# Centring the rows as they leave PSUM, whole-height transposing products, other gate sums for three pairs, and a new order

## Chip, core and metric

The kernel runs on one core of a Trainium2 chip. The metric is the device time of one execution in microseconds. The kernel before took 188.77 us, the median of three runs (188.55 to 188.9). The engines named below are PE (TensorE: matrix products), DVE (VectorE), ACT (ScalarE), POOL (GpSimd) and SP, whose queue issues nearly all transfers.

## What is computed

Four batches of eight heads, each a complex gated linear recurrence over 768 tokens of width 48, followed by a layer norm and a two-layer network over the 384 joined columns:

```
mag = np.sqrt(a_re * a_re + a_im * a_im)
scale = np.minimum(mag, 0.999) / (mag + 1e-06)
...
for t in range(S):
    new_re = ar * S_re - ai * S_im
    new_im = ar * S_im + ai * S_re
    kv = np.einsum('bhd,bhe->bhde', k[:, :, t], v[:, :, t])
    S_re, S_im = (new_re + kv, new_im)
    y[:, :, t] = np.einsum('bhd,bhde->bhe', q[:, :, t], S_re)
...
mu = np.mean(x, axis=-1, keepdims=True)
var = np.mean((x - mu) ** 2, axis=-1, keepdims=True)
xn = (x - mu) / np.sqrt(var + 1e-06) * g_ln
ch = np.maximum(xn @ w_ch1, 0.0) @ w_ch2
return (x + ch).astype(np.float32)
```

## The kernel before

The tokens are cut into 24 chunks of 128 (index `n`), taken two at a time as 12 pairs (`P`), three pairs to a batch. For a pair the gates come first: `are` and `aim` are loaded, ACT takes a logarithm and a reciprocal (`ln`, `iv`), DVE or POOL form the ratio `r` and its square `r2`, and `u`, `l`, `lc` give the log of the decay, `th` the angle. PE sums both along the tokens with triangular matrices of ones, `dec` (L466) and `ph` (L481): a partition holds two neighbouring tokens (`j` 0 and 1), so each of the two chunks of a pair needs two products with `u_e` or `u_th`. `ph` starts with a product that brings in the carried angle. ACT turns the sums into `e`, `en`, `sin`, `cos`. Then `ke`, `qe`, `ks`, `qs` scale keys and queries; `kT` and `qT` (L581) are PE transposes of eight heads, copied out as `ksT`, `qsT`. Some chunks take a transposing DMA on SP instead. `am` (L604) makes the scores, DVE masks them (`atm`), `gm` and `G` carry the state, and `y` (L665) is the output of the recurrence. `dps` (L563) moves the last decay row into a column: eight products with one moving column, whose rows are partitions 96 to 127. `decc` copies it out.

For the network, `x` (L677) copies `y` out of PSUM as bf16 on ACT or DVE, `bn` (L680) takes mean and variance of `x` on DVE, and `xtr`, `xT` transpose it. The mean is taken out through the first weights: `wp` (L375) forms the column means of the scaled weights on PE, and `wc` (L381) scales `w1b` and subtracts them. That is done once. `mm1` (L718) multiplies, in six halves to a pair; `relu` leaves PSUM on ACT or DVE; `mm2` (L744) multiplies again, in three parts to a chunk. `ot` scales by `rstd` and adds `x`: in one DVE operation from PSUM (L761), or as `oa` on ACT (L751) followed by an addition on POOL (L759). `st` stores.

`warm` products at the start compute nothing that is used.

`PLAN` (L39) is a written-out list of all operations. An operation `name:E` goes to the queue of engine `E` in the order of the list, a digit after it names its PSUM bank, and `@other` makes it wait for `other`, so that POOL and DVE take turns. Each engine works through its own queue in order. `RINGS` says how many buffers a tile has.

Of the kernel before, what the change touches and what calls it, by code (L numbers as in the profile page):

```python
# [9 lines left out]
FP32 = mybir.dt.float32  # L10
# [24 lines left out]

ENGINES = {"P": "PE", "A": "ACT", "V": "DVE", "G": "POOL", "S": "SP"}
# [27 lines left out]
sin.3.0:A6 are.5.0:S mm1.0.1.1:P0 atm.3:V2 wl.1:G@mm1.0.1.0 v.1:A qt.3.0:P6 vf.2.0:S relu.0.1:A0 ke.2.0.0:G wc.2.2:V5
gm.2:P2 y.2:P3 G.2:V2 cos.3.0:A6 ke.2.0.1:G mm1.0.2.0:P0 wc.0.2:V4 x.2:A3 y.3:P5 qe.2.0.0:G wc.0.0:V4 gm.3:P2 x.3:A5
mm1.0.2.1:P0 wc.0.1:V4 ks.2.0.1:G xtr.2:P3 xtr.3:P5 xT.2:A3 mm1.0.0.0:P6 xT.3:V5 relu.0.2:A0 bn.1:V mm1.1.0.1:P4
ks.2.0.0:V mm1.0.0.1:P6 bn.0:V qs.2.0.0:G@ks.2.0.0 mm1.1.2.0:P0 relu.0.0:V6 tab.log.6:A u.3.0:A kT.4:P3 mm1.1.0.0:P4
one:G ksT.4:V3 ln.4.0:A mm1.1.2.1:P0 qs.2.0.1:V relu.1.0:A4 gs.3:V2 mm1.1.1.1:P6 l.3.0:V iv.4.0:A kT.5:P2 qT.5:P5
relu.1.2:A0 lc.3.0:V mm1.1.1.0:P6 aim.5.0:S ksT.5:V2 G.3:G@lc.3.0 qT.4:P3 qsT.5:V5 relu.1.1:A6 dec.3.0:P0 qsT.4:V3
vf.2.1:S am.5:P4 e.3.0:A0 r.4.0:V am.4:P6 en.3.0:A0 dps.3:P3 atm.5:V4 mm2.1.0:P2 are.6.0:S r2.4.0:A mm2.1.1:P2  # L70
atm.4:V6 vf.3.0:S u.4.0:A mm2.1.2:P2 mm2.0.0:P0 rstd.0:A l.4.0:V ln.5.0:A k.3.0:S mm2.0.1:P0 lc.4.0:V iv.5.0:A
mm2.0.2:P0 decc.3:V3 k.3.1:S ot.1:V2 dec.4.0:P6 v.2:A r.5.0:G@lc.4.0 bn.3:V mm2.3.0:P5 e.4.0:A6 ot.0:V0 q.3.1:S
gm.4:P1 bn.2:V y.4:P3 en.4.0:A6 mm2.3.1:P5 q.3.0:S r2.5.0:G G.4:V1 ln.6.0:A mm2.3.2:P5 x.4:V3 vf.3.1:S iv.6.0:A y.5:P0
bn.4:V xtr.4:P1 mm2.2.0:P4 ke.3.0.0:G k.4.1:S x.5:V0 u.5.0:A xT.4:V1 mm2.2.1:P4 ke.3.0.1:G st.0:S xtr.5:P0 mm2.2.2:P4
xT.5:V0 rstd.1:G l.5.0:V k.4.0:S mm1.2.1.1:P0 tab.trig.7:A th.5.0:A mm1.2.1.0:P0 qe.3.0.1:V aim.6.0:S th.4.0:A
qe.3.0.0:V mm1.2.2.1:P2 relu.2.1:A0 qs.3.0.1:V q.4.0:S mm1.2.2.0:P2 ks.3.0.0:V q.4.1:S ph.4.0:P6 qs.3.0.0:V
relu.2.2:A2 ks.3.0.1:V are.7.0:S qT.6:P0 lc.5.0:V car.4.0:A6 bn.5:V kT.6:P1 ke.4.0.1:G@lc.5.0 abs.4.0:A6 ph.5.0:P2
ot.2:V4 q.5.1:S oa.3:A5 ke.4.0.0:G@lc.5.0 ksT.6:V1 sin.4.0:A6 kT.7:P4 qsT.6:V0 r.6.0:G vf.4.0:S qT.7:P1 cos.4.0:A
ksT.7:V4 mm1.2.0.0:P6 vf.4.1:S abs.5.0:A2 qsT.7:V1 mm1.2.0.1:P6 v.3:G sin.5.0:A2 dec.5.0:P0 relu.2.0:V6 st.2:S
cos.5.0:A qe.4.0.1:G am.7:P4 am.6:P2 th.6.0:A atm.7:V4 are.8.0:S ks.4.0.0:G gm.6:P6 mm2.4.0:P7 G.6:A6 mm2.4.1:P7  # L80
r2.6.0:A st.1:S atm.6:V2 mm2.4.2:P7 ot.3:G aim.7.0:S dps.4:P4 gm.7:P6 qe.4.0.0:G st.3:S decc.4:V4 y.7:P3 G.7:V6 y.6:P2
tab.log.8:A u.6.0:A mm2.5.0:P5 x.7:V3 rstd.2:G ks.4.0.1:V mm2.5.1:P5 x.6:A2 q.5.0:S en.5.0:A0 l.6.0:V xtr.6:P6 k.5.1:S
xtr.7:P2 kT.9:P4 v.4:A xT.6:V6 mm2.5.2:P5 xT.7:V2 lc.6.0:V e.5.0:A0 vf.5.1:S qs.4.0.1:V mm1.3.1.0:P2 ln.7.0:A ot.4:V7
qs.4.0.0:G@qs.4.0.1 dec.6.0:P0 ot.5:V5 mm1.3.1.1:P2 iv.7.0:A bn.7:V mm1.3.0.0:P6 ksT.9:A4 relu.3.1:V2 r.7.0:G qsT.8:S
qT.9:P5 en.6.0:A0 mm1.3.0.1:P6 qsT.9:V5 k.5.0:S e.6.0:A0 kT.8:P2 relu.3.0:V6 qe.5.0.1:G am.9:P4 st.4:S ln.8.0:A
mm1.3.2.1:P0 qe.5.0.0:G q.6.0:S atm.9:V4 r2.7.0:A mm1.3.2.0:P0 qs.5.0.0:G iv.8.0:A gm.8:P3 ph.6.0:P6 aim.8.0:S G.8:V3
u.7.0:A ksT.8:V2 y.9:P4 q.6.1:S relu.3.2:V0 qs.5.0.1:G mm2.7.0:P5 st.5:S gm.9:P3 mm2.7.1:P5 bn.6:V k.6.0:S
tab.trig.9:A th.7.0:A am.8:P0 ke.5.0.1:G mm2.6.0:P2 car.6.0:A6 atm.8:V0 rstd.3:G sin.6.0:A6 are.9.0:S mm2.7.2:P5
x.9:A4 mm2.6.1:P2 ke.5.0.0:V abs.6.0:A6 k.6.1:S gs.9:V3 y.8:P0 ks.5.0.0:V vf.5.0:S mm2.6.2:P2 x.8:A0 l.7.0:V dps.6:P1
qsT.10:S qT.11:P0 xtr.9:P3 lc.7.0:V xtr.8:P4 qsT.11:A0 ph.7.0:P6 ks.5.0.1:V ot.6:V2 q.7.1:S r.8.0:G@ks.5.0.1 xT.9:A3  # L90
kT.11:P0 ot.7:V5 xT.8:A4 kT.10:P2 st.6:S bn.8:V abs.7.0:A6 mm1.4.0.0:P4 ksT.10:V2 sin.7.0:A6 ke.6.0.0:G aim.9.0:S
mm1.4.0.1:P4 bn.9:V decc.6:A1 mm1.4.2.1:P2 th.8.0:A ke.6.0.1:G ksT.11:V0 mm1.4.2.0:P2 cos.6.0:A relu.4.0:V4 G.9:G
k.7.0:S mm1.4.1.0:P0 relu.4.2:A2 mm1.4.1.1:P0 ks.6.0.1:V vf.6.1:S v.5:V mm2.8.0:P4 relu.4.1:A0 car.7.0:V6 vf.7.1:S
ks.6.0.0:G@v.5 am.10:P2 am.11:P6 atm.10:V2 gm.10:P5 k.7.1:S mm2.8.1:P4 qe.6.0.1:G mm2.8.2:P4 G.10:V5 are.10.0:S
tab.log.10:A rstd.4:A ln.9.0:A atm.11:V6 qe.6.0.0:G kT.12:P2 st.7:S dec.7.0:P0 iv.9.0:A qs.6.0.0:V y.10:P3 vf.6.0:S
en.7.0:A0 qs.6.0.1:V y.11:P5 ph.8.0:P6 ksT.12:V2 r.9.0:G@qs.6.0.1 x.10:A3 qsT.13:S x.11:V5 e.7.0:A0 qT.12:P3 ot.8:V4
r2.8.0:A xtr.11:P2 xtr.10:P0 qsT.12:V3 mm2.9.0:P1 k.8.0:S ke.7.0.1:G u.8.0:A xT.11:V2 mm2.9.1:P1 xT.10:V0 st.8:S
bn.11:V ke.7.0.0:G mm2.9.2:P1 q.7.0:S bn.10:V am.12:P4 ks.7.0.1:G ot.9:V1 mm1.5.1.1:P2 tab.trig.11:A th.9.0:A
# [109 lines left out]
def kernel(  # L208
# [14 lines left out]
    C = 128  # L223
# [47 lines left out]
    def eng(name):  # L271
        return g.ops[name].eng
# [46 lines left out]

    def c_uth():  # L320
        nc.vector.tensor_scalar(out=u_th, in0=u_e, scalar1=INV2PI, scalar2=None, op0=ALU.mult)

    def c_pick():
        nc.gpsimd.memset(pick, 0.0)
        for row in (HALF, C - 1):
# [491 lines left out]
```

## Time and profile before

| | us |
|---|---|
| median of three runs | 188.77 |
| the profiled execution, its own time | 188.55 |
| its span, first to last instruction | 186.8 |
| busy in the span: PE / DVE / ACT / POOL | 180.8 / 157.9 / 152.3 / 98.7 |
| granted TensorE clock | 1.0 throughout |

The span is 1.75 us shorter than the execution's own time. A line of a group gives the line of the kernel, engine, operation, output and input, shapes, count, then busy time, mean time of one in ns, and the engine's idle time before them. Mean times of one overlap: an engine starts the next instruction before the last has written everything, so 24 of 551 ns take less than 24 times that. The end of a matrix product is modelled, and PE is called busy until then, so the spacing of a long row of products says more about PE than its busy share.

### The profile page before, as it was taken

The numbers are of one execution on the slowest core, as the hardware profiler recorded it, in microseconds if no ns is written. First come the engines' busy times: TensorE is split into PE (matmuls) and PEld (weight loads), VectorE is DVE, ScalarE is ACT, GpSimd is POOL, SyncE is SP. The second block draws the span as 40 slices with busy tenths as digits, with TensorE's granted clock in tenths as the row PEclk, the third lists the DMA queues.
The fourth block names the chain that finished last, engine by engine and source line by source line (L and its number), as shares of the span: only waits on it lengthen the run. The fifth ranks groups of instructions, "written<-read, shape, count | busy, mean of one in ns | idle before, by whom it ended". The sixth has DMA issues, their size and how long they took to land.

```text
span 186.8 us, 5113 instructions
## 1 busy us (share of the span) xinstructions
PE 180.8 (97%) x2031; PEld 139.8 (75%) x2032; DVE 157.9 (84%) x287; ACT 152.3 (81%) x219; POOL 98.7 (53%) x117
## 2 busy tenths in 40 slices
PE   5999899999999999999999999999999999999993
PEld 2365467689967887796897887886986978888783
DVE  0458999999999898999989998999898988879523
ACT  3999999888999999999799989999999843533450
POOL 8531227968109389598476944577943066130320
PEclk9999999999999999999999999999999999999999
DMA  5999999999978986769969999999997789779132
GB/s 157 281 234 214 254 192 216 235 249 199 219 148 171 255 177 194 166 146 228 231 147 231 230 227 207 173 252 222 206 218 139 149 177 228 173 139 170 39 112 86
DMA packets 124536, 35.93 MB, mean 192 GB/s; under 512 B 120544, under 2 KB 123744, under 8 KB 124512
## 3 DMA queue, kind: packets, MB, share of 16 engines
q1 hardware_dynamic: 123712, 33.24, 82.1%
q0 software_dynamic: 800, 2.36, 6.8%
q8 instruction: 16, 0.26, 0.6%
q14 instruction: 8, 0.07, 0.1%
HBM read 28.31 MB, written 4.72 MB: 177 GB/s over the span
## 4 chain that ended last, share of the span: by engine, by line
PE 76%; SPq 7%; DVE 7%; ACT 4%; issue 2%; DMA 2%; POOL 1%; POOLq 0%
PE banks L722 23%; PE banks L746 22%; SPq L397 6%; PE banks L584 5%; PE banks L780 5%; PE banks L607 5%; PE banks L489 3%; PE banks L470 2%; PE banks L668 2%; PE banks L631 2%; PE banks L671 2%; DVE w1b L381 2%; PE banks L689 2%; PE banks L485 2%; DMA k<-in_k_dram 2%
## 5 line engine op out<-in xcount | busy, mean ns | idle before, releaser
L746 PE MATMUL banks<-w2b,h 128*128 128x384 bf16 (+2 forms) x300 | 52.7, 319 | 0.0
L722 PE MATMUL banks<-xT,w1b 128*128 128x256 bf16 x432 | 51.5, 273 | 0.0
L722 PEld LDWEIGHTS <-w1b 128*128 128x128 bf16 x432 | 46.3, 114 | 1.1
L746 PEld LDWEIGHTS <-h 128*128 128x128 bf16 x300 | 27.0, 98 | 13.7 <-ACT h L734 0.2
L734 ACT ACTIVATE h<-banks 128x1024 bf16<-128x1024 f32 x24 | 24.4, 1023 | 10.9 <-PE banks L722 10.9
L288 DVE TENSOR_TENSOR atm<-banks,mask 128x1024 bf16<-128x1024 f32 x24 | 29.1, 1218 | 2.6 <-PE banks L607 2.4
L288 POOL TENSOR_TENSOR ke<-k,en 128x384 bf16<-128x384 f32 x19 | 17.2, 919 | 13.4 <-ACT h L734 5.1
L288 POOL TENSOR_TENSOR r<-aim,are 128x768 f16<-128x768 f32 x8 | 14.6, 1820 | 12.7 <-ACT are L443 9.7
L785 ACT ACT_TABLE_LOAD x15 | 19.2, 1283 | 1.0 <-PEq L801 0.8
L780 PE MATMUL banks<-u_e 128*128 128x512 f16 x55 | 16.1, 438 | 2.3 <-POOL u_e L316 2.2
L736 DVE TENSOR_SCALAR h<-banks 128x1024 bf16<-128x1024 f32 x12 | 14.6, 1216 | 4.0 <-PE banks L722 4.0
L288 POOL TENSOR_TENSOR qe<-q,e 128x384 bf16<-128x384 f32 x14 | 12.7, 917 | 7.6 <-DMA q<-in_q_dram 4.0
L759 POOL TENSOR_TENSOR ot<-ot,x 128x384 f32<-128x384 f32 x9 | 8.1, 914 | 16.0 <-ACT ot L751 11.4
L607 PE MATMUL banks<-qsT,ksT 128*128 128x128 bf16 x192 | 14.2, 219 | 0.0
L681 DVE BATCH_NORM_STATS2 stats<-x 128x6 f32<-128x384 bf16 x24 | 13.2, 551 | 0.3 <-ACT x L283 0.2
L607 PEld LDWEIGHTS <-ksT 128*128 128x128 bf16 x192 | 11.9, 98 | 1.7 <-DVE atm L288 0.2
L780 PEld LDWEIGHTS <-u_e 128*128 128x128 f16 x55 | 5.9, 109 | 9.1 <-issue 4.2
L459 DVE SCALAR_TENSOR_TENSOR l<-r,w 128x768 f16<-128x768 f16 (+1 forms) x13 | 12.1, 931 | 0.2 <-ACT r L455 0.2
L288 POOL TENSOR_TENSOR qs<-qe,trig 128x768 bf16<-128x768 bf16 x6 | 9.8, 1644 | 4.3 <-DVE qs L288 2.2
L441 ACT ACTIVATE w<-are 128x768 f32<-128x768 f32 (+1 forms) x13 | 10.2, 791 | 2.3 <-DMA are<-in_a_re_dram 2.3
L489 PE MATMUL banks<-th,u_th 128*128 128x384 f16 (+1 forms) x52 | 11.8, 313 | 0.0
L668 PE MATMUL banks<-v,atm 128*128 128x48 bf16 x192 | 11.8, 183 | 0.0
(96 smaller groups left out, 386.1 us busy)
## 6 DMA issues: line engine op xcount, KB each, us to landing
k<-in_k_dram SPq DMA_DIRECT2D x24, 192.0 KB, 3.7
vf<-in_v_dram SPq DMA_DIRECT2D x24, 192.0 KB, 4.3
q<-in_q_dram SPq DMA_DIRECT2D x24, 192.0 KB, 4.2
out_dram<-ot SPq DMA_DIRECT2D x23, 192.0 KB, 3.1
are<-in_a_re_dram SPq DMA_DIRECT2D x11, 384.0 KB, 4.6
aim<-in_a_im_dram SPq DMA_DIRECT2D x11, 384.0 KB, 4.7
w1b<-in_moe_w_ch_dram POOLq DMA_DIRECT2D x1, 1152.0 KB, 9.6
w2b<-in_moe_w_ch_dram POOLq DMA_DIRECT2D x1, 1152.0 KB, 11.4
```

Source lines behind the costliest of these rows:

```text
L288: {"DVE": nc.vector, "POOL": nc.gpsimd}[eng(name)].tensor_tensor(**kw)
L459: nc.vector.scalar_tensor_tensor(out=S_("l"), in0=S_("r2"), scalar=0.5, in1=S_("w"), op0=ALU.mult, op1=ALU.add)
L489: nc.tensor.matmul(heads(ps[:, c]), lhsT=u_th[:, c, j], rhs=step(T("th", P), j), start=False, stop=(j == R - 1), skip_group_check=True)
L607: nc.tensor.matmul(ps[:, h], lhsT=T("ksT", n)[:, h], rhs=T("qsT", n)[:, h], start=True, stop=True)
L668: nc.tensor.matmul(ps[:, h], lhsT=T("atm", n)[:, h], rhs=T("v", P)[:, c, h], start=True, stop=nfirst)
L681: nc.vector.bn_stats(out=T("stats", n), in_=T("x", n))
L722: nc.tensor.matmul(ps[:, jj], lhsT=w1b[:, dc, ts(gi, JG * C)].rearrange("k (p j) -> k j p", j=JG)[:, jj], rhs=T("xT", P)[:, dc].rearrange( ...
L734: act(out=dst, in_=src, func=AF.Relu)
L736: nc.vector.tensor_scalar(out=dst, in0=src, scalar1=0.0, scalar2=None, op0=ALU.max)
L746: nc.tensor.matmul(bank(f"o.{N}")[:, ws], lhsT=T("h", P)[:, j, ts(c, C)], rhs=w2b[:, j, ws], start=(j == 0), stop=(j == NJ - 1))
L780: g.add(f"warm.w{i}", lambda i=i: nc.tensor.matmul(bank(f"warm.w{i}"), lhsT=u_e[:, 0, 0], rhs=u_e.rearrange("p c j t -> p (c j t)"), start ...
L785: g.add(f"tab.{nm}.{i}", lambda tab=tab: nc.scalar.preload_act_table_set(tab))
```

## The change

1. `bn` reads `y` from PSUM. `x` now waits for `bn` and is written as mean minus `y`. The first weights are only scaled, by minus `g_ln`; `wp`, `wgc` and `cmean` are gone, and `wc` has no PSUM operand.
2. The end of a chunk becomes `ob` (scale and add the mean, out of PSUM, on ACT or DVE) and `ot` (subtract `x`, on DVE or POOL) for pairs 0 to 10. Pair 11 keeps one DVE operation, with `xr` restoring `y` beforehand.
3. `dps` uses all 128 rows.
4. For pairs 9, 10 and 11 a partition holds one token of each chunk. `dec` and `ph` then need one product for the first chunk and two for the second, with new matrices `u_ec`, `u_thc`. Their `are` and `aim` come in two transfers each, of 48 numbers in a run instead of 96.
5. The order is new, and some operations go to another engine. Five `warm.w` fewer, three `warm` more.

```diff
+WHOLE = {9, 10, 11}
...
+uth:V q.0.1:S pad.qs.1:G@uth iv.1.0:A car0.1:G@uth aim.0.0:S ident:G@uth ln.0.0:A ln.0.1:A pad.ks.0:G iv.0.0:A one:G
+zdec:G are.2.0:S pad.ks.1:G iv.0.1:A gln:S r.0.1:V r.1.0:V q.0.0:S tab.trig.1:A th.0.1:A th.1.0:A aim.2.0:S r.0.0:V
...
+cos.1.0:A4 ks.0.0.0:V wl.0:G@ks.0.0.0 v.0:V q.2.0:S warm.w45:P0 warm.w46:P0 warm.w47:P0 warm.18:P0 warm.19:P0 kT.0:P0
...
+gm.1:P4 ph.2.0:P6 G.1:V4 atm.0:V2 r.3.0:G qT.2:P4 qsT.2:V4 warm.23:P0 y.0:P1 tab.trig.5:A sin.2.0:A6 qT.3:P0 bn.0:V1
+y.1:P2 v.1:G th.3.0:A qt.2.0:P6 qsT.3:V0 am.2:P4 r2.3.0:G x.0:A1 bn.1:V2 cos.2.0:A6 warm.24:P0 ph.3.0:P0 atm.2:V4
+x.1:A2 k.2.1:S gm.2:P7 pad.ks.2:G car.3.0:A0 xtr.0:P2 xtr.1:P3 G.2:V7 xT.0:A2 am.3:P4 are.4.0:S xT.1:A3 y.2:P6
+wc.0.2:V wc.0.0:V sin.3.0:A0 wc.0.1:V gm.3:P7 atm.3:V4 mm1.0.0.0:P2 aim.4.0:S qe.2.0.0:G@wc.0.1 qt.3.0:P0 bn.2:V6
+mm1.0.0.1:P2 vf.2.1:S cos.3.0:A0 wl.1:G@bn.2 y.3:P4 wc.1.2:V wc.2.0:V wc.1.0:V relu.0.0:A2 vf.2.0:S wc.1.1:V wc.2.2:V
+bn.3:V4 mm1.0.1.1:P0 ke.2.0.1:G@wc.2.2 x.2:A6 mm1.0.1.0:P0 x.3:V4 xtr.2:P6 wc.2.1:V qe.2.0.1:V xtr.3:P2 mm1.0.2.1:P4
+xT.2:A6 xT.3:V2 ke.2.0.0:G@qe.2.0.1 gs.3:V7 mm1.0.2.0:P4 mm1.1.2.1:P2 ks.2.0.0:V tab.log.6:A u.3.0:A ks.2.0.1:V
...
+    def c_uec():
+        nc.gpsimd.memset(u_ec, 1.0)
+        nc.gpsimd.affine_select(out=u_ec[:, 0], in_=u_ec[:, 0], pattern=[[1, C]],
+                                compare_op=ALU.is_ge, fill=0.0, base=0, channel_multiplier=-1)
+    def c_uthc():
+        nc.vector.tensor_scalar(out=u_thc, in0=u_ec, scalar1=INV2PI, scalar2=None, op0=ALU.mult)
...
-            g.add(f"wc.{jb}.{ec}", lambda jb=jb, ec=ec, o=o: nc.vector.scalar_tensor_tensor(
-                out=w1b[:, ec, ts(jb, 512)], in0=w1b[:, ec, ts(jb, 512)], scalar=gln[:, ds(ec, 1)],
-                in1=bank(o), op0=ALU.mult, op1=ALU.subtract), needs=[o], ps=(o, 1))
+            g.add(f"wc.{jb}.{ec}", lambda jb=jb, ec=ec: nc.vector.tensor_scalar(
+                out=w1b[:, ec, ts(jb, 512)], in0=w1b[:, ec, ts(jb, 512)], scalar1=gln[:, ds(ec, 1)],
+                scalar2=-1.0, op0=ALU.mult, op1=ALU.mult), needs=["gln", "wl.0"])
...
+            def sums(pairs, chunks, c):
+                if P in WHOLE:
+                    return [(chunks[:, 1 if j < c else 0], j, j == c) for j in range(c + 1)]
+                return [(pairs[:, c, j], j, j == R - 1) for j in range(R)]
...
+                    for j in range(R):
+                        nc.sync.dma_start(out=step(T(nm, P), j), in_=ap[b][hs].rearrange(
+                            "h (c p) d -> p c h d", p=C)[:, pp * R + j])
...
-                                     lhsT=T("e", P)[96:C, R - 1, ts(h, D)],
-                                     rhs=ident[96:C, C - 1:C], start=True, stop=True)
+                                     lhsT=T("e", P)[:, R - 1, ts(h, D)],
+                                     rhs=ident[:, C - 1:C], start=True, stop=True)
...
-                nc.vector.bn_stats(out=T("stats", n), in_=T("x", n))
+                nc.vector.bn_stats(out=T("stats", n), in_=bank(f"y.{n}")[:, 0:DM])
                 nc.vector.bn_aggr(out=T("mv", P)[:, c], in_=T("stats", n))
...
+            def f_x(n, c):
+                if eng(f"x.{n}") == "ACT":
+                    act(out=T("x", n), in_=bank(f"y.{n}")[:, 0:DM], func=AF.Identity, scale=-1.0,
+                        bias=T("mv", P)[:, c, 0:1])
+                else:
+                    nc.vector.tensor_scalar(out=T("x", n), in0=bank(f"y.{n}")[:, 0:DM],
+                                            scalar1=T("mv", P)[:, c, 0:1], scalar2=-1.0,
+                                            op0=ALU.subtract, op1=ALU.mult)
...
+            def f_xr(n, c):
+                {"DVE": nc.vector, "POOL": nc.gpsimd}[eng(f"xr.{n}")].tensor_scalar(
+                    out=flat(T("gt", n - 10)), in0=T("x", n), scalar1=-1.0,
+                    scalar2=T("mv", P)[:, c, 0:1], op0=ALU.mult, op1=ALU.add)
...
+                        if eng(f"ob.{n}") == "ACT":
+                            act(out=o, in_=y, func=AF.Identity, scale=rs, bias=mean)
+                        else:
+                            nc.vector.tensor_scalar(out=o, in0=y, scalar1=rs, scalar2=mean,
+                                                    op0=ALU.mult, op1=ALU.add)
...
+                    add(f"ot.{N}", lambda n=n: tt(
+                        f"ot.{n}", out=T("ot", n), in0=T("ot", n), in1=T("x", n), op=ALU.subtract),
```

280 lines of the change are left out of this document (130 added, 150 removed).

## The prediction

> **What bounds the kernel now.** First the windows, in three stages (window, then busy time of PE, weight loads, DVE, ACT, POOL; clock; DMA share), cut where pair 1's first layer is under way (47) and where pair 9's begins (156).
>
> ```profile
> 20.00:47.00 27.00, 26.17 (x323) 19.56 (x323) 26.40 (x50) 24.76 (x37) 16.57 (x16) 1.00 1.07 226
> 47.00:156.00 109.00, 108.89 (x1304) 87.68 (x1302) 102.08 (x187) 101.27 (x142) 66.05 (x65) 1.00 0.93 197
> 156.00:184.00 28.00, 27.96 (x314) 23.50 (x311) 19.46 (x32) 9.89 (x18) 7.70 (x10) 1.00 0.60 131
> ```
>
> From 47 on PE is never idle by its row; DVE and ACT have 6.9 and 7.7 us free in the middle stage and much more in the last. Before 47 DVE is full, 26.40 of 27.00, and PE's row there holds products that only warm. Then the chain of waits (start, length, what):
>
> ```profile
> 34.95 1.40 DVE w1b L381 x2
> ...
> 43.15 2.68 PE banks L722 x24
> ...
> 51.83 0.35 PE banks L565 x8
> ...
> 71.56 1.95 PE banks L746 x12
> ...
> 83.36 0.20 PE banks L631 x8
> ...
> 92.04 0.89 PE banks L584 x16
> ...
> 150.14 0.65 PE banks L470 x4
> ...
> 156.53 3.93 PE banks L722 x36
> ...
> 180.03 3.94 PE banks L746 x36
> ...
> 184.00 0.35 DVE ot L761
> ```
>
> The reader is to see the spacing: 36 products of the first layer in 3.93 us are 109 ns each, 12 of the second in 1.95 are 162, 16 transposes in 0.89 are 56, four gate sums in 0.65 are 162. With these prices all products of the list that do real work sum to 158.9 us (my sum, each operation at the price of its kind). Of these 21.2 stand in PE's queue ahead of pair 1's first `mm1`, 137.7 behind it. That `mm1` is the second of the four halves at 43.15, so it begins at 43.8; from there to 184.0 are 140.2, and 2.4 is all that holes and dearer products can hold. So the time is **the moment the first layers can start, set by DVE's queue, plus PE's remaining products, plus 2.8 us behind the last one**. What leaves DVE or ACT after 47 buys nothing; what leaves PE's queue counts in full, as long as DVE and ACT keep up.
>
> **The change, part by part.**
>
> *Gate sums of pairs 9 to 11.* `dec` loses one of four products a pair, `ph` one of four beside the carry: six at 162 ns, **-0.98**, all behind pair 1's start. Against it stand six more transfers on SP's queue, and the runs of these loads are halved, 6 x 1024 more packets.
>
> ```profile
> q1 hardware_dynamic: 123712, 33.24, 82.1%
> ...
> ACT w L441 <- DMA are<-in_a_re_dram: 2.3, 1, 2.3
> ```
>
> A packet takes 82.1% of 186.8 us of 16 engines over 123712, 19.8 ns; so they cost between nothing (time goes by bytes) and 6144 x 19.8 / 16 = 7.6 us of the engines' time in all, 2.5 a pair. Three transposing transfers fewer give some back. I take 0: only the first `are` was ever waited for (2.3 us at the start), the others land far ahead of `ln`. Without that cover a pair's gates come up to 2.5 later.
>
> *`dps` over all rows.* The products themselves are no cheaper; what goes is what stands around them.
>
> ```profile
> L565 PEld LDWEIGHTS <-e 32*48 32x48 bf16 x64 | 2.2, 95 | 1.8 <-issue 1.5 <-ACT e L474 0.2
> L631 PE MATMUL banks<-v,ks 128*128 128x48 bf16 x160 | 7.3, 183 | 0.1
> ```
>
> Eight take 0.28 on the chain where eight full-height ones (L631) take 0.20, and ahead of them the weight loads wait 1.5 us in six places for nothing but issue. Two of the eight `dps` fall before that point and don't count. The other six: at least 6 x 0.08 = 0.5, at most 0.5 + 1.5 = 2.0. Part of that wait is covered by the products still running; I take **-1.0**, between the two and nearer the lower.
>
> *Transposes.* Two more `qT` (eight at 56 ns, 0.45 each) replace transposing transfers, and one more `xtr` (three at 56): **+1.06**.
>
> *The first weights.* `wp` (nine products of 512 columns) goes, and `wc` loses its PSUM operand.
>
> ```profile
> L377 PE MATMUL banks<-w1b,gc 128*128 128x512 bf16 x8 | 2.4, 379 | 0.1
> L381 DVE SCALAR_TENSOR_TENSOR w1b<-w1b,gln,banks 128x512 bf16<-128x512 bf16 x9 | 6.2, 740 | 0.0
> L321 DVE TENSOR_SCALAR u_th<-u_e 128x512 f16<-128x512 f16 x1 | 0.3, 287 | 0.0
> L462 DVE TENSOR_SCALAR l<-l x13: 259/354/912, 13.3 to 148.9; 128x768 f16<-128x768 f16 x11, 128x384 f16<-128x384 f16 x2
> ```
>
> `wp` is 1.9 us of PE, but before 47, where DVE sets the pace: worth 0 by itself. `wc` falls from 740 to about 300 (a scalar operation of that size and 16 bits took 287), 6.7 to 2.7 us; bounds 287 and 912, which one `lc` (L462) took beside POOL work. The order holds POOL's next multiplications behind `wc.0.1` and `wc.2.2`, so I stay at 300. In the Trainium skill, SBUF — State Buffer, section Who interferes with whom says that a DVE operation in a two-port mode and a POOL one shut each other out for a whole instruction, which speaks against this edit, since the old form read PSUM; at 912 each `wc` by it would be 8.2 us, 5.5 more than my sum has. The one long `lc` of thirteen agrees that it happens, not that it is usual.
>
> *The start as a whole.* Do the 4.0 us that `wc` gives up reach the start? I multiplied every DVE operation ahead of pair 1's first `mm1` by its mean: 37.2 us before, 37.2 after. What fills the room is `bn` of four chunks instead of none, `x.3`, two more key multiplications for pair 1 and one more copy of transposed keys. PE has 19.2 us of real work there without `wp`, and 19.9 after: the sixth half of pair 0's `mm1` now stands ahead. So the start ends when it did, with 0.65 less of PE's work left, **-0.65**. The first weights' load is a cover to watch: it moves behind `ks.0.0.0`.
>
> ```profile
> 21.77 1.00 POOL L352 DMA_DIRECT2D w1b<-in_moe_w_ch_dram  x1 [5.58 <-DVE ke L288]
> ...
> DMA to landing us min/median/max: 9.6/9.6/9.6
> ...
> 25.45 0.68 DVE L285 COPY qsT<-banks 128x1024 bf16<-128x1024 bf16 x1
> ...
> 37.40 1.40 DVE L381 SCALAR_TENSOR_TENSOR w1b<-w1b,gln,banks 128x512 bf16<-128x512 bf16 x2
> ```
>
> `ks.0.0.0` ends 17.0 us into DVE's work, which was reached at 25.5; the load would land at 35 to 36. `wc.0.2` stands 29.7 us in, reached at 37.4. The margin is 1.3 to 2.3 us. Bounds of the start come from the windows ahead of it (columns as above):
>
> ```profile
> 0.00:10.00 10.00, 7.78 (x24) 3.10 (x25) 2.63 (x6) 6.82 (x10) 6.50 (x26) 1.00 0.87 217
> 10.00:20.00 10.00, 10.00 (x74) 5.99 (x72) 6.94 (x14) 9.52 (x17) 1.91 (x2) 1.00 1.05 223
> ```
>
> DVE has 7.4 + 3.1 us free there. I allow 2 us earlier, if the order uses a fifth of that, and 2 later, if a load or `iv.0.1`, which the first `r` now waits for, comes late.
>
> *Centring and the ends of chunks.* These land on DVE, ACT and POOL.
>
> ```profile
> L283 ACT CAST x<-banks 128x384 bf16<-128x384 f32 x14 | 6.7, 478 | 4.0 <-PE banks L671 2.9 <-PE banks L668 1.1
> L751 ACT ACTIVATE ot<-banks,rstd 128x384 f32<-128x384 f32 x9 | 5.2, 582 | 3.7 <-PE banks L746 2.0 <-issue 1.7
> L761 DVE SCALAR_TENSOR_TENSOR ot<-banks,rstd,x 128x384 f32<-128x384 f32 x14 | 8.3, 607 | 2.2 <-PE banks L746 2.2
> L681 DVE BATCH_NORM_STATS2 stats<-x 128x6 f32<-128x384 bf16 x24 | 13.2, 551 | 0.3 <-ACT x L283 0.2
> L682 DVE BATCH_NORM_AGGREGATE mv<-stats 128x2 f32<-128x6 f32 x24 | 4.4, 182 | 0.8
> L759 POOL TENSOR_TENSOR ot<-ot,x 128x384 f32<-128x384 f32 x9 | 8.1, 914 | 16.0 <-ACT ot L751 11.4
> ```
>
> `bn` from PSUM I take at its 551, with 607 (DVE's nearest PSUM row) as the upper end. The new wait puts 551 + 182 = 0.73 us between `y` and `x`, and so ahead of `xtr`, `xT` and `mm1`. Behind a waiting `bn` stands all of DVE's queue, next of all `atm`, for which PE's `y` waits; behind `x` on ACT stand `sin`, `cos` and the `relu`. I cost this at 0, since the list puts other PE work between `y` and `mm1` (chunk 18's `y` and `xtr` have parts of two `mm2` between them); without the cover it is 0.73 for each of eleven pairs, 8 us. The totals: 14 `ob` on ACT in place of 9 `oa`, at 582, +2.9; eight `ob` on DVE, four more `x`, and more copies and multiplications there, +14.4, against three `relu` at 1.22 and others fewer, -10.4, and `wc`, -4.0: DVE stays within 1 us of its total. ACT, with three `relu`, seven `car` for four and two table loads more, but fewer `v`, `x`, `ksT` and `rstd`, gains 2.7. POOL gains 6 on 98.7 of 186.8. None of them is the bound by its total: 0 for all.
>
> *Sum* behind pair 1's start: -0.98 - 1.0 + 1.06 - 0.65 = **-1.57**. The profiled execution's span 186.8 becomes 185.2, its time 188.55 becomes 187.0; against the median, 0.2 higher, **187.2 us**. `warm` products fill holes only: 0.
>
> **The rivals.**
>
> *ACT becomes the bound in the middle stage (slower).* From pair 1's first `mm1` to pair 9's the list gives ACT 113.6 us before and 116.6 after, by the same means; busy time is 0.92 of that, so 101.27 becomes 104.0. PE's share of the stage falls by 1.4, and by 0.8 for `dps`: 109 to 106.8. ACT may then stand idle 2.8 us at no cost, where it stood 7.7. From 4.4 the gain is eaten; at 7.7 the time is 187.2 + 4.9 = 192.1; half of that excess gives 190.0, my figure, with 188.9 to 192.1. For it: `x` waits for one more engine. Against it: most of the 7.7 is waiting for PE itself, as `x` does in the rows above, and shrinks when PE is the slower one. In the Trainium skill, Perfetto Trace Analysis, section Identifying the Most-Contended Engine says to judge PE by the share of its weight loads and the other engines by occupancy; by it the middle stage has PE at 80% (87.68 of 109) and DVE and ACT at 94 and 93%, so that they are the bound already, and 2.7 us more on ACT would give 188.77 + 2.7 = 191.5. The even spacing of 109 and 162 ns with no idle PE speaks against that reading.
>
> *The start ends earlier (faster still).* Of the 10.4 us that DVE had free before 20 the order takes 2: 187.2 - 2 = 185.2. For it: `wc` no longer waits for PE. Against it: DVE has as much to do up to there.
>
> *Nothing arrives (no change).* From 112.81 the chain leaves PE and comes back to it at 126.95, by way of DVE and ACT:
>
> ```profile
> 112.81 1.11 issue
> 113.91 0.55 DVE ks L288
> 114.46 0.47 DVE G L288
> 114.93 0.46 DVE r L288
> ...
> 126.95 0.62 PE banks L584 x8
> ```
>
> There PE was fed just in time. What is saved ahead of it, 0.65 at the start, two thirds of 1.0 for four `dps` and 0.16 for pair 9's `ph`, is waited out in this stretch; behind it stand -0.82 for the other gates and -0.33 for two `dps`, against +1.06 of transposes, which leaves 188.77 - 0.1 = 188.7. For it: this stretch. Against it: the order there is new.
>
> **How the numbers follow.** Forecast 0.52; ACT the bound 0.23; the early start 0.12; nothing arrives 0.13. Under 0.2% (0.4 us) a measurement of this kernel can't tell from no change. Faster: 0.49 of the forecast, the early start, and 0.02 of the last, 0.63. Same: 0.02 of the forecast, 0.11 of the last and 0.01 of ACT's case, 0.14. Slower: the rest, 0.23. The range: low 185.0, the early start with the larger `dps` bound left out; high 190.3, past the middle of ACT's case; 0.07 lies below and 0.12 above. The forecast's own range is 186.1 to 188.4.
>
> **What would show it.** Right: PE without a hole from 47 on; the L565 loads no longer idle for issue; `wc` near 300 ns, done before pair 1's `mm1`; that `mm1` at about 44 with 0.65 us more work done ahead of it; five products a pair in `ph`. ACT's idle time in the middle stage under 4. Wrong: holes of PE ended by `x`, `xT`, `relu` or `atm`; `wc` at 700 or more; a first `mm1` after 40 because the weights landed late; `are` waited for in pairs 9 to 11.

## The result, and the profile after

The kernel after took **193.23 us** (193.21 to 193.99), the kernel before beside it 188.66 (188.46 to 189.59): a ratio of 1.0234, 95% interval 1.0207 to 1.0261. It is slower by 3.9 to 4.9 us (the interval times 188.66); 187.2 was predicted, and the range ended at 190.3. The span of its profiled execution is 191.4 us, 4.6 more than before.

The windows of the kernel after, same stretches as before (window, then busy time of PE, weight loads, DVE, ACT, POOL; clock; DMA share):

```profile
20.00:47.00 27.00, 25.51 (x314) 19.88 (x313) 26.17 (x58) 24.26 (x35) 15.00 (x14) 1.00 1.05 214
47.00:156.00 109.00, 107.17 (x1277) 84.86 (x1275) 105.83 (x188) 103.50 (x136) 72.81 (x74) 1.00 0.92 192
156.00:184.00 28.00, 26.89 (x317) 22.48 (x315) 20.23 (x34) 12.34 (x19) 12.26 (x13) 1.00 0.55 123
```

The start is as before. From 47 on PE, which was idle for 0.15 us in the two later windows before, is now idle for 2.9, and more time is lost in short pauses that its busy share hides. Counted from the starts of the products (the distance from one start to the next, less the usual distance behind a product of that shape, where the difference is over 0.06 us), there are 6.0 us of pauses behind pair 1's first `mm1` against 1.6 before. DVE is at 105.83 of 109.

The groups of the kernel after that answer to those of before (output and input, shapes, count, then busy time, mean ns of one, idle time before):

```profile
L292 DVE TENSOR_TENSOR ot<-ot,x 128x384 f32<-128x384 f32 x14 | 13.9, 1000 | 2.3 <-ACT ot L776 2.3
L682 DVE BATCH_NORM_STATS2 stats<-banks 128x6 f32<-128x384 f32 x24 | 13.3, 556 | 1.8 <-PE banks L675 1.7
L776 ACT ACTIVATE ot<-banks,mv,rstd 128x384 f32<-128x384 f32 x14 | 9.4, 670 | 1.1 <-issue 1.1
L692 DVE TENSOR_SCALAR x<-banks,mv 128x384 bf16<-128x384 f32 x14 | 8.4, 609 | 0.3
L689 ACT ACTIVATE x<-banks,mv 128x384 bf16<-128x384 f32 x10 | 5.8, 578 | 4.4 <-DVE mv L683 4.4
L778 DVE TENSOR_SCALAR ot<-banks,rstd,mv 128x384 f32<-128x384 f32 x8 | 5.4, 669 | 0.0
L374 DVE TENSOR_SCALAR w1b<-w1b,gln 128x512 bf16<-128x512 bf16 x9 | 2.8, 366 | 0.0
L569 PEld LDWEIGHTS <-e 128*48 128x48 bf16 x64 | 2.2, 100 | 1.9 <-issue 1.5 <-ACT en L478 0.3
```

Two things stand out. The weight loads of `dps` still idle 1.5 us for issue. And `ot` on DVE takes 1000 ns in the mean, where the one-operation `ot` of before took 607. The tile's own view of `ot` gives its spread (count, minimum, median, maximum), in the kernel after:

```profile
L292 DVE TENSOR_TENSOR ot<-ot,x x14: 550/997/1844, 56.9 to 185.2; 128x384 f32<-128x384 f32 x14
```

The same view of the kernel before:

```profile
L761 DVE SCALAR_TENSOR_TENSOR ot<-banks,rstd,x x16: 350/608/618, 55.8 to 184.0; 128x384 f32<-128x384 f32 x14, 128x256 f32<-128x256 f32 x1, 128x128 f32<-128x128 f32 x1
```

The same shape takes 550 or 1844: something outside the instruction decides. The timeline of the kernel after around its longest one (start, length, engine, what; in brackets the idle time before and what ended it), the rows of DVE, POOL and PE:

```profile
158.84 0.56 DVE L292 TENSOR_TENSOR ks<-ke,trig 128x768 bf16<-128x768 bf16 x1
...
159.31 0.55 DVE L292 TENSOR_TENSOR G<-banks,dec 128x384 bf16<-128x384 f32 x1
159.57 1.64 POOL L292 TENSOR_TENSOR ks<-ke,trig 128x768 bf16<-128x768 bf16 x1 [8.10 <-DVE ks L292]
159.78 1.84 DVE L292 TENSOR_TENSOR ot<-ot,x 128x384 f32<-128x384 f32 x1
...
160.55 0.82 PE L742 MATMUL banks<-xT,w1b 128*128 128x256 bf16 x6
...
161.17 1.23 POOL L292 TENSOR_TENSOR qe<-q,e 128x384 bf16<-128x384 f32 x1
...
161.55 0.55 DVE L292 TENSOR_TENSOR G<-banks,G 128x384 bf16<-128x384 f32 x1
162.02 0.80 DVE L292 TENSOR_TENSOR ot<-ot,x 128x384 f32<-128x384 f32 x1
162.15 0.36 PE L635 MATMUL banks<-v,ks 128*128 128x48 bf16 x8 [0.78 <-DVE G L292]
```

POOL's `ks` starts 0.21 us ahead of `ot` and ends at 161.21; `ot` ends at 161.62, 0.41 later. `G.20` stands behind `ot.16` in DVE's queue, `gm.21` on PE waits for `G.20`: the largest pause of PE, 0.78 by this row. At 66.70 the same: `ot.3` takes 1.62 beside POOL's `r`, which ends at 67.90, again 0.42 ahead of the end of `ot`, and the copies of keys and queries behind it make PE wait 0.61. Of the 14 `ot`, nine start while POOL is well into an operation on two tiles; all nine are long, and each ends 0.41 or 0.42 us after that operation. The five that start first, as POOL ends, or while it stands still take 550 to 559.

In the Trainium skill, SBUF — State Buffer, section Who interferes with whom says that a DVE instruction with two inputs in SBUF contends with a POOL instruction that reads SBUF. These rows agree: 550 to 559 for those five, up to 1844 beside POOL. The prediction took the section's other rule, on two-port modes, and weighed it against `wc`; eight of the nine `wc` took 323 to 349 ns and one 553.

### The profile page after: what moved, and what is told of

It is laid out like the page before. It is cut to its first block, busy times and chain, and to the rows that moved or that the text cites. A ratio compares the mean times of both kernels' runs of the same rounds, so it can differ in the third digit from the quotient of the medians.

```text
span 191.4 us, 5141 instructions
## 1 busy us (share of the span) xinstructions
PE 179.6 (94%) x2034; PEld 138.7 (72%) x2034; DVE 165.2 (86%) x303; ACT 158.1 (83%) x213; POOL 107.5 (56%) x128
## 5 line engine op out<-in xcount | busy, mean ns | idle before, releaser
L754 ACT ACTIVATE h<-banks 128x1024 bf16<-128x1024 f32 x27 | 27.4, 1021 | 11.4 <-PE banks L742 11.1
L292 POOL TENSOR_TENSOR ke<-k,en 128x384 bf16<-128x384 f32 x15 | 14.3, 953 | 13.3 <-DVE qs L292 6.3
L292 POOL TENSOR_TENSOR qe<-q,e 128x384 bf16<-128x384 f32 x17 | 16.8, 993 | 7.9 <-DVE l L466 3.1
L292 POOL TENSOR_TENSOR qs<-qe,trig 128x768 bf16<-128x768 bf16 x9 | 14.9, 1664 | 2.8 <-DVE l L463 2.5
L292 DVE TENSOR_TENSOR ot<-ot,x 128x384 f32<-128x384 f32 x14 | 13.9, 1000 | 2.3 <-ACT ot L776 2.3
L806 PE MATMUL banks<-u_e 128*128 128x512 f16 x50 | 13.6, 416 | 2.3 <-POOL u_e L320 2.2
L682 DVE BATCH_NORM_STATS2 stats<-banks 128x6 f32<-128x384 f32 x24 | 13.3, 556 | 1.8 <-PE banks L675 1.7
L756 DVE TENSOR_SCALAR h<-banks 128x1024 bf16<-128x1024 f32 x9 | 10.9, 1219 | 2.3 <-PE banks L742 2.3
L292 POOL TENSOR_TENSOR ks<-ke,trig 128x768 bf16<-128x768 bf16 x4 | 6.5, 1640 | 9.9 <-DVE ks L292 8.1
L672 PEld LDWEIGHTS <-atm 128*128 128x128 bf16 x192 | 10.7, 96 | 1.8 <-DVE atm L292 1.2
```

Of the source, the lines that this page charges most:

```text
L292: {"DVE": nc.vector, "POOL": nc.gpsimd}[eng(name)].tensor_tensor(**kw)
L672: nc.tensor.matmul(ps[:, h], lhsT=T("atm", n)[:, h], rhs=T("v", P)[:, c, h], start=True, stop=nfirst)
L682: nc.vector.bn_stats(out=T("stats", n), in_=bank(f"y.{n}")[:, 0:DM])
L754: act(out=dst, in_=src, func=AF.Relu)
L756: nc.vector.tensor_scalar(out=dst, in0=src, scalar1=0.0, scalar2=None, op0=ALU.max)
L806: g.add(f"warm.w{i}", lambda i=i: nc.tensor.matmul(bank(f"warm.w{i}"), lhsT=u_e[:, 0, 0], rhs=u_e.rearrange("p c j t -> p (c j t)"), start ...
```

## The experiments

Three theories stood at the start. **The shared port**: `ot`, split off from the scaling, has two operands in SBUF, waits for POOL, and holds up what is behind it in DVE's queue. **The new wait**: `x` waits for `bn`. **More work**: `ob`, `x` and `bn` from PSUM are simply longer. All ratios below are to the kernel before, run beside.

### One part alone, in the kernel before

`dps` over all rows:

```diff
-  lhsT=T("e", P)[96:C, R - 1, ts(h, D)], rhs=ident[96:C, C - 1:C]
+  lhsT=T("e", P)[:, R - 1, ts(h, D)],    rhs=ident[:, C - 1:C]
```

> The kernel before with the dps products over all 128 rows, nothing else. The prediction's step: 1.0 us less (188.66 -> 187.7), the issue idle ahead of the dps weight loads gone (1.5 us before). Rival, read from the profile after, where that idle still stands at 1.5 us: no change, 188.7 +- 0.3, the dps group's idle for issue stays near 1.5.

Measured: 188.6 us, ratio 0.9987 (0.9968 to 1.0006). The row of its weight loads, by groups:

```profile
L565 PEld LDWEIGHTS <-e 128*48 128x48 bf16 x64 | 2.2, 100 | 1.8 <-issue 1.5 <-ACT e L474 0.2
```

Nothing went: the idle 1.5 is where it was, and a load takes 100 ns where it took 95. By the interval the step is worth between 0.6 us less and 0.1 more, so the 1.0 of the prediction is ruled out.

The gate sums of pairs 9 to 11 alone (`WHOLE` with its functions, in the order of before):

```diff
+WHOLE = {9, 10, 11}
-... pad.ks.1:G ... gs.9:V3 ...
+... pad.ks.1:G uec:G ... gs.9:V3 uthc:V ...
```

> The kernel before with the gate sums of pairs 9 to 11 one token a partition (their loads in two transfers, the two new matrices made on POOL and DVE at the start, behind the last key pad and behind gs.9), nothing else. The prediction's step: six products of 162 ns, 0.98 us less (187.7). Rival one: what is saved is waited out near 113 to 127, or the six added transfers delay SP's queue: 188.4 to 189.0. Rival two: the extra make of the matrices delays the start, over 189.

Measured: 189.19 us, 1.0006 (0.9977 to 1.0034), no change. In the order of before, six products fewer buy nothing that can be told, and where their 0.98 us went is not shown. This comes back below in the new order.

### Does `x` behind `bn` cost?

A constant column takes the place of the mean, so that `x` needs nothing of `bn`; on DVE `x` also moves ahead of `bn` in the order.

```diff
-  scale=-1.0, bias=T("mv", P)[:, c, 0:1])
+  scale=-1.0, bias=gln[:, 0:1])
-  needs=[f"bn.{n}"], uses=[("x", n), ("mv", P)]
+  needs=[f"y.{n}", "gln"], uses=[("x", n)]
```

> The kernel after, where x takes a constant column in place of the mean and so does not wait for bn; on DVE x stands ahead of bn. The rows are not centred by the right mean; every instruction is still there. Theory that the new wait of x for bn makes the holes: time 193.2 -> 190.5 or less, holes behind xtr gone. Shared-port theory: 192.3 to 193.4, the ot on DVE still near 1000 ns, and the holes of 0.94 and 0.77 us still there.

Measured: 193.2 us, 1.022 (1.0187 to 1.0253), the same as the kernel after. But the edit did not free `x` on ACT, as its row in the groups shows:

```profile
L688 ACT ACTIVATE x<-banks,gln 128x384 bf16<-128x384 f32 x10 | 5.8, 577 | 4.4 <-DVE stats L681 4.4
```

`x` no longer reads anything that `bn` writes, and still idles 4.4 us for it: both read the same PSUM bank, and the second reader waits for a semaphore that the first one raises. So `x` was moved ahead of `bn` in the order on ACT too.

> The kernel after, where x takes a constant column in place of the mean and stands ahead of bn in the order on both engines, so that no x is behind a bn (in the run before, those on ACT still idled 4.4 us for the statistics). The rows are not centred by the right mean. Theory that the wait of x for bn makes holes: x on ACT no longer idles for DVE, time 193.2 -> 191.5 or less. Shared-port theory alone: 192.5 to 193.5.

Measured: 196.19 us, 1.0393 (1.0364 to 1.0423), 3 us slower than the kernel after, where 191.5 or less would have spoken for the wait. Now `bn` is the one behind:

```profile
L681 DVE BATCH_NORM_STATS2 stats<-banks 128x6 f32<-128x384 f32 x24 | 13.4, 559 | 5.2 <-ACT x L688 5.1
```

One of the two readers waits in either order. With `x` first on DVE alone (the run before this one) nothing changed; the 3 us come with the ten `x` on ACT, for which DVE, the fuller engine, now idles. The order of the change is the better one here. What `x` and `bn` side by side would give could not be tried this way and stays open.

### Is it the two operands from SBUF?

First the operands alone: the 14 `ob` write back into their bank, and `ot` reads PSUM and `x`.

```diff
+  o = y if eng(f"ot.{n}") == "DVE" else T("ot", n)      # ob, in place
-  ot: in0=T("ot", n)
+  ot: in0=bank(f"o.{n}")[:, 0:DM]
```

> The kernel after, where the 14 ob whose ot is on DVE write back into their PSUM bank and those ot read PSUM and x, so only one operand from SBUF. Eleven of these ot stand earlier in the order, ahead of the next use of their bank. Same number of instructions and the same values. Shared-port theory: every ot near 600 ns beside POOL work (now 550 to 1844, mean 1000), DVE 4 to 6 us less busy, PE's holes behind 40 us from 6.0 to about 2.5, time 193.2 -> 189.5 (188.5 to 191). Rival, the wait of x for bn makes the holes: ot shorter but time 192.5 to 193.5. Rival, the larger ob and x (670, 578 to 609 ns) make it: also 192.5 or more.

Measured: 195.76 us, 1.0365 (1.0332 to 1.0398). The mechanism came as expected and the time did not. Its group of `ot`, and then its middle window:

```profile
L293 DVE TENSOR_TENSOR ot<-banks,x 128x384 f32<-128x384 f32 x14 | 7.6, 549 | 2.3 <-ACT banks L778 2.3
```

```profile
47.00:156.00 109.00, 103.83 (x1247) 83.48 (x1245) 99.54 (x181) 100.30 (x132) 69.94 (x74) 1.00 0.91 189
```

`ot` takes 549 in the mean and at most 558, also where it starts in the middle of a POOL operation on two tiles (at 57, 77, 92 and 136 us), and DVE is 6.3 us less busy. But a bank is held until `ot`, and whoever takes it next waits: by its waits PE idles 5.7 us in all for an `ot`. In the timeline of this kernel the largest case is the gate sum of pair 9, which waits for `ot.10` to give up bank 4:

```profile
124.48 0.55 DVE L293 TENSOR_TENSOR ot<-banks,x 128x384 f32<-128x384 f32 x1
...
125.08 0.48 PE L475 MATMUL banks<-l,u_ec 128*128 128x384 f16 x2 [1.46 <-DVE ot L293]
```

So the next edit keeps place, waits and banks, and puts a statistics instruction, which reads one tile, in the place of the subtraction of two. The 14 chunks go out without `x`. (That the statistics also write less is not what counts: the `ot` of the run above wrote the whole tile to SBUF and stayed short.)

```diff
-  tt(f"ot.{n}", out=T("ot", n), in0=T("ot", n), in1=T("x", n), op=ALU.subtract)
+  nc.vector.bn_stats(out=odd, in_=T("ot", n))            # on DVE
```

> The kernel after, where each of the 14 ot on DVE is replaced, at its place, by a statistics instruction over the same 384 numbers of ot (one operand from SBUF, nothing written to ot). The rows are left without x in those 14 chunks. Same count of instructions, same waits for ob, no bank held longer. Shared-port theory: each takes 550 ns whatever POOL does, DVE 5 to 6 us less busy, the holes of 0.94 and 0.77 us gone, time 193.2 -> 190.0 (189 to 191.2). Rival, the time is set by the wait of x for bn and the number of instructions on DVE: 192.3 or more.

Measured: **188.41 us**, 0.9985 (0.9969 to 1.0001): 4.8 us less than the kernel after. The statistics in the tile's view:

```profile
L786 DVE BATCH_NORM_STATS2 odd<-ot x14: 528/553/562, 57.6 to 181.3; 128x6 f32<-128x384 f32 x14
```

The windows of this kernel, columns as above:

```profile
47.00:156.00 109.00, 108.94 (x1317) 87.68 (x1315) 103.53 (x192) 105.17 (x139) 71.04 (x74) 1.00 0.94 198
156.00:184.00 28.00, 27.60 (x315) 23.12 (x313) 18.82 (x34) 11.77 (x16) 11.74 (x13) 1.00 0.55 120
```

The timeline of the same stretch as above, POOL's rows, then DVE's, then PE's:

```profile
157.22 1.65 POOL L292 TENSOR_TENSOR ks<-ke,trig 128x768 bf16<-128x768 bf16 x1 [8.10 <-DVE ks L292]
158.82 0.93 POOL L292 TENSOR_TENSOR qe<-q,e 128x384 bf16<-128x384 f32 x1
```

```profile
157.43 0.55 DVE L786 BATCH_NORM_STATS2 odd<-ot 128x6 f32<-128x384 f32 x1
157.90 0.54 DVE L292 TENSOR_TENSOR G<-banks,G 128x384 bf16<-128x384 f32 x1
158.36 0.55 DVE L786 BATCH_NORM_STATS2 odd<-ot 128x6 f32<-128x384 f32 x1
```

```profile
158.21 0.82 PE L743 MATMUL banks<-xT,w1b 128*128 128x256 bf16 x6
158.86 0.36 PE L636 MATMUL banks<-v,ks 128*128 128x48 bf16 x8
```

The statistics start 0.21 us after POOL's `ks`, as `ot.16` did, and take 553 ns instead of 1844; `G.20` starts 0.47 later instead of 1.77, and PE goes from the first layer into `gm.21` without a pause. Counted as above, PE's pauses are 1.4 us, where they were 6.0: 4.6 of the 4.8 us. POOL gains too: its `qe` takes 0.93 instead of 1.23. PE is busy 108.94 of 109, with the longer `x`, `ob` and `bn` all in place and ACT at 105.17: those are not the cause, and neither is the wait of `x`.

Both edits together:

> Both edits of the two runs above together. If the two costs are separate and the port is most: 189.5 to 190.5, near the run with the one-operand ot alone. If they cover each other (each alone shows nothing, since the other still holds DVE): clearly below both, under 189.5.

Measured: 191.91 us, 1.0167 (1.0144 to 1.019). This is above both ranges that were expected. The order with `x` first costs 3.0 us beside the long `ot` and 3.5 beside the short one; neither cost hides the other.

### The row path of before in the new order

`x` copies `y`, ahead of `bn`; `ot` on DVE is one operation from PSUM at the place of `ob`.

```diff
-ob.5:A1 ... ot.5:V ... bn.6:V0 x.6:V0
+ot.5:V1 ... x.6:V0 bn.6:V
```

> The kernel after with the row path of before: x copies y and stands ahead of bn, bn reads x, the 14 ot on DVE are one operation from PSUM at the place of their ob (which goes), the eight on POOL keep a scaling ob, no xr. The weights stay only scaled, so the mean is left in. Order, gate sums, dps, transposes as after. The prediction's sum without its centring: 187.2 (186.5 to 188). If the new order itself is the loss: 191 or more. In between, the row path explains 193.2 less what is measured.

Measured: 194.11 us, 1.0287 (1.0258 to 1.0315). That is 191 or more, which was to speak against the new order; but `x` is first here too: DVE idles 5.4 us for the `x` on ACT, as it did 5.1 in the run above that cost 3 us. So it settles nothing about the order. The one-operand kernel does: in it the new order runs with PE busy for 108.94 of the 109 us of the middle stage.

### Can the gain be had with all values right?

DVE subtracts `x` straight from PSUM where `ob` stood (one operand from SBUF), and ACT adds the mean where `ot` stood; for the nine chunks whose `ob` was on ACT, then for all 14.

```diff
-ob.16:A7 ... ot.16:V
+ob.16:V7 ... ot.16:A
+  nc.vector.scalar_tensor_tensor(out=o, in0=y, scalar=rs, in1=T("x", n), op0=ALU.mult, op1=ALU.subtract)
+  act(out=T("ot", n), in_=T("ot", n), func=AF.Identity, bias=T("mv", P)[:, c, 0:1])
```

> The kernel after, where for the nine chunks with ob on ACT and ot on DVE the two swap: DVE scales out of PSUM and subtracts x in one operation at the place of ob (one operand from SBUF), and ACT adds the mean to the row in SBUF at the place of ot. All values as before; the other five ot on DVE still have two operands from SBUF. Shared-port theory: the nine take near 607 ns beside POOL, holes behind 100 us go, those near 58 and 68 us stay; 190 to 191 if DVE does not stall at the earlier places. Rival, what counts is that ot stands late in DVE's queue and not in front of atm and G: 193 or more.

> As the run before, for all 14 chunks with ot on DVE (five additions of the mean more on ACT, five scalings fewer on DVE). Shared-port theory: no long ot is left, 188.4 to 189.5, as the one-operand run, if ACT has room for about 3 us more; with ACT the bound 190 or more, and holes ended by relu or x on ACT.

Measured: 192.03 (1.0177, 1.0145 to 1.021) and 192.52 (1.0201, 1.0164 to 1.0238). The new DVE operation takes 604 and 607 ns in the mean and at most 620, as expected, and in the second kernel DVE is 6.2 us less busy in the middle stage; still only 0.7 to 1.2 us come back. In the first the pause of 0.62 near 69 us, behind an `ot` that was left as it was, is still there. In the second other pauses appear: the longest in its middle stage, 0.75 at 96.75, is ended by ACT's `sh`, another of 0.46 by its `trig`, with ACT at 105.01 of 109. So the second outcome of the expectation came, though not by `relu` or `x`.

Then `ot` as it is, moved within DVE's queue to where POOL stands still:

```diff
-bn.9:V7 ot.5:V bn.8:V0 x.9:V7 ob.6:V1 ks.5.0.0:V xT.9:V3 ks.5.0.1:V
+bn.9:V7 bn.8:V0 x.9:V7 ob.6:V1 ks.5.0.0:V xT.9:V3 ot.5:V ks.5.0.1:V
...
-ke.11.0.0:V qe.11.0.0:V ke.11.0.1:V ks.11.0.1:V G.19:V5 ot.16:V G.20:V1 ot.17:V
+ot.17:V ke.11.0.0:V qe.11.0.0:V ke.11.0.1:V ot.16:V ks.11.0.1:V G.19:V5 G.20:V1
```

> The kernel after with 13 of the 14 ot on DVE moved in DVE's queue, by at most a few microseconds, to places where POOL stands still in the one-operand run: beside the ke, qe, ks, qs of DVE that already take turns with POOL (ot.6 ahead of qs.5.0.0, ot.14 ahead of v.9, ot.17 ahead of ke.11.0.0 and so on; st.5 and st.14 follow). No work changed, all values as before, every ot still with two operands from SBUF. Shared-port theory: most ot at 550, DVE 4 to 6 us less busy, 188.4 to 190. Rival, it is the additional DVE work itself (ob, ot, bn from PSUM) that makes the holes: 192 or more.

Measured: 191.51 us, 1.0158 (1.0127 to 1.0189). In the tile's view of this kernel:

```profile
L290 DVE TENSOR_TENSOR ot<-ot,x x14: 546/550/558, 61.3 to 184.8; 128x384 f32<-128x384 f32 x14
```

No `ot` is long any more, with two operands from SBUF and no work changed: that settles that it is the meeting with POOL that makes them long. But the time is 3.1 us over the one-operand kernel. Either the places cost, or the two-operand form costs in another way. The next run has the moved places with the one-operand instruction:

> The order of the run before (ot moved to places where POOL stands still), with the one-operand statistics instruction in place of each of the 14 ot on DVE; those 14 chunks are left without x. Neither kernel has a long ot on DVE. If the 3 us between the run before (191.5) and the one-operand run at the old places (188.4) are the price of the places: 191 to 191.8. If something else of the two-operand form costs (POOL held up, the store that waits for ot): 188.2 to 189.

Measured: 191.91 us, 1.0166 (1.0119 to 1.0212), the same as with the two-operand `ot`. **It is the places.** Its timeline on DVE and, below, on PE shows one such case and, in its last line, the end of another:

```profile
88.74 0.55 DVE L784 BATCH_NORM_STATS2 odd<-ot 128x6 f32<-128x384 f32 x1
89.20 0.54 DVE L290 TENSOR_TENSOR ks<-ke,trig 128x768 bf16<-128x768 bf16 x1
89.66 0.55 DVE L290 TENSOR_TENSOR qs<-qe,trig 128x768 bf16<-128x768 bf16 x1
90.13 0.55 DVE L784 BATCH_NORM_STATS2 odd<-ot 128x6 f32<-128x384 f32 x1
90.60 0.54 DVE L290 TENSOR_TENSOR qs<-qe,trig 128x768 bf16<-128x768 bf16 x1
91.06 0.67 DVE L777 TENSOR_SCALAR ot<-banks,rstd,mv 128x384 f32<-128x384 f32 x1
```

```profile
91.78 0.61 PE L587 MATMUL banks<-ident,ks 128*128 128x128 bf16 x8 [0.77 <-DVE ot L777]
...
172.41 0.61 PE L610 MATMUL banks<-qsT,ksT 128*128 128x128 bf16 x8 [0.94 <-DMA qsT<-qs]
```

Two of the statistics, 0.47 us each by their spacing, now stand among the multiplications ahead of `ob.7` (91.06), one of which came behind it before; `ob.7` frees the bank that the key transposes take, and PE waits 0.77 for it. At 172.41 it goes by way of POOL and SP: `ks.11.0.1` has the two statistics of chunks 16 and 17 ahead of it, POOL's part of that pair waits for it by its `@`, a transposing transfer of `qsT` for POOL, and the scores `am` on PE wait 0.94 us for the transfer.

Last, `ot` on POOL:

```diff
-ot.2:V ... ot.1:V ... ot.3:V ...
+ot.2:G ... ot.1:G ... ot.3:G ...
```

> The kernel after with 13 of the 14 ot of DVE on POOL, at the same places of the order (ot.21 stays). All values as before. POOL has 36 us free of 109 in the middle stage and takes 13 x 0.91 = 11.8 more, DVE is freed of all long ot. Shared-port theory: DVE as in the one-operand run or better, so 188.5 to 190 if POOL's own queue holds nothing up; if what stands behind ot on POOL (r, ke, qe) is late, 191 or more with holes ended by DVE work that waits for POOL.

Measured: 192.76 us, 1.0206 (1.0167 to 1.0245). POOL goes to 82.76 of 109 and is still not full, but its queue is in order too: two `ot` at 160.46, 1.79 us together, stand ahead of its `qe` and `qs`, and PE waits 2.1 us for the transposing transfers of `qsT` behind these, where it waited for none in the one-operand kernel. The meeting with DVE's own two-operand work goes on from the other side: DVE's `qe` takes 802 ns where it took 553. None of these kernels beats the kernel before.

### The gate sums in the new order

> The one-operand run (188.41) with pairs 9 to 11 summed as the other pairs, the two new matrices still made. The prediction's term for the gates: 0.98 more, 189.4, first mm1 of pair 11 0.8 later. If the gates are worth nothing here too, as beside the kernel before: 188.2 to 188.7.

The edit is `WHOLE = set()` in the one-operand kernel. Measured: 189.87 us, 1.0056 (1.0037 to 1.0076), against 0.9985: 0.7% or 1.3 us more, with about 0.5 to either side from the two intervals. The starts of the products in the two traces agree better: behind pair 1's first `mm1` they hold 0.96 us more of products here and the same 1.4 us of pauses. So the six products are worth their price, 0.98, in this order; why they bought nothing in the order of before stays open.

## Why the prediction was wrong

It failed at one step of *Centring and the ends of chunks*: "**DVE stays within 1 us of its total**". The sum has no term for `ot` on DVE: 14 stood there before and 14 after, so the split form was taken at nothing more than the 607 ns of the one-operation form, and no reason is given. That form read PSUM and one tile in SBUF; the split form reads two tiles in SBUF and waits for POOL. DVE went from 157.9 to 165.2 us of busy time; 14 x (1000 - 607) is 5.5 of that. The rest is smaller things of the same step: 14 `x` at 609 instead of some 550 (0.8), eight `ob` at 669 instead of some 600 (0.6), `wc` at 366 instead of 300 (0.6). And the wait does not only fill DVE: it stands ahead of `G`, `qsT` and `xT`, which PE waits for. Taken out at its place, it gives back 4.8 us, and DVE is then busy for 158.9 us, 1.0 more than before: the rest of the step held in sum, with the statistics at 553 ns in the place of the 607. The kernel could have warned: by `@` the order makes POOL's work take turns with DVE's `ke`, `qe`, `ks` and `qs`, for which its code gives the reason "turns at the shared port", and nowhere with an `ot` of DVE.

**The other terms.** From pair 1's first `mm1` to the end of the last `ot` the traces give, with the pauses counted as above (one profiled execution of each kernel, us):

| kernel | first `mm1` of pair 1 | to the end of the last `ot` | pauses of PE | the rest, products |
|---|---|---|---|---|
| before | 43.67 | 140.68 | 1.6 | 139.06 |
| after | 43.36 | 144.53 | 6.0 | 138.54 |
| one-operand | 44.03 | 139.96 | 1.4 | 138.53 |
| one-operand, gate sums as before | 43.51 | 140.92 | 1.4 | 139.49 |

The one-operand kernel's last `ot` ends at 183.03 + 0.96 = 183.99; the row, from its timeline, has the two last together:

```profile
183.03 0.96 DVE L792 SCALAR_TENSOR_TENSOR ot<-banks,rstd,gt 128x256 f32<-128x256 f32 x2 [0.66 <-issue]
```

The sum of the prediction was -1.57. Without `dps` it is -0.57, and the products went down by 0.52 and 0.53. So the account of PE's products held, in the kernel after too; what came on top there are 4.4 us more of pauses. By term:

- **Gates, -0.98:** 0.96 by the table, 1.3 with 0.5 to either side by the times; 0 in the order of before. The rival "nothing arrives" does not explain that 0, since it lets 0.82 of this term through. The loads cost nothing that shows: in the kernel after ACT waits for `are` once, 2.2 us at the start. (Before, DVE also waited 7.2 us for the first `aim`, which the prediction passes over.)
- **`dps`, -1.0:** 0 as far as can be told. The idle time of its weight loads does not hang on their height: 1.5 us with 32 rows and with 128.
- **Transposes, +1.06, and the start, -0.65:** not tried alone; they are in the products of the table. The start itself came as forecast, 43.36 and 44.03 against 43.67, with one half of pair 0's `mm1` more ahead of it. `wc` took 366 ns; all nine were done before pair 1's first `mm1`, though pair 0's waited for them twice, 0.4 us in all.
- **`bn` ahead of `x`, 0:** held as far as it was tried; the other order is 3 us worse.
- **Behind the last product, 2.8:** 0.6 more in the one-operand kernel and 1.0 in the kernel after, which the prediction left out. The records of SP at the end show part of it: SP waits for six pairs of semaphores in a fixed sequence, and the last store's is first in it now and was last before, so the other waits, some 0.07 us each and one of 0.38 in the kernel after, follow the last landing. The rest of it was not looked for.

**The rivals.** *ACT becomes the bound* gave 190.0 (its own rule, half of 4.9 on 187.2, gives 189.7) and fell: with 105.17 of 109 on ACT, more than the 103.50 of the kernel after, PE was busy for 108.94 of 109. The time came out slower, but by DVE. ACT did gain more than the 2.7 of the sum, 152.3 to 158.1, since `ob` and `x` were priced by shorter forms there too (670 and 578 against 582 and 478). *The start ends earlier* by 2 us did not come either. The Trainium skill, Perfetto Trace Analysis, section Identifying the Most-Contended Engine, judges PE by its weight loads and the other engines by occupancy. By that DVE or ACT is the bound in the kernel before, the kernel after and the one-operand kernel. The last, with 95 and 96% on them, 80% on the weight loads (87.68 of 109) and yet 108.94 of 109 on PE, speaks against it there; the kernel after, with 97% on DVE, speaks for it.

## What to carry to other kernels

Splitting an operation can change where its operands lie, and with it whom it waits for: before pricing the new part by the old row, look whether a row with the same number of operands in SBUF stands beside the other engine's work. On an engine that is as full as DVE is here (97% of the middle stage) and works its queue in order, look at what stands behind a late instruction, not only at its length. And a tuned order is worth a few microseconds that move with any instruction (here 3 to 3.5 for the moved places and for `x` first): an edit that removes a stall, and also shifts a place, must be run against one that only shifts the place.

## What the runs showed of the hardware

- DVE's 128x384 subtraction of two SBUF tiles took 550 ns alone and up to 1844 beside a POOL multiplication of 1640; all nine long ones ended 0.41 or 0.42 us after POOL's end. With one operand from PSUM it took 524 to 558, in the middle of such a POOL operation 524 to 548, and a statistics instruction over one SBUF tile 528 to 562. POOL's next instruction was held too (1.23 instead of 0.93 us).
- Two engines that read the same PSUM bank were put one behind the other, in whichever order the list gave them, without any value passing between them (4.4 us of idle time for ten `x`, 5.1 for the `bn` the other way round). In the trace it is a wait for a semaphore that the first one raises; what the chip would do without it was not tried.
- DVE's scaling from PSUM with two per-row scalars took 669 ns, on ACT 670, where the forms with one scalar took 606 on DVE (in the kernel with the old row path) and 582 on ACT.
